# Windowed attention and maxout FFN on one core: the loads of chunk 1 and the transposes of chunk 3

## The chip, the cores and the metric

The kernel runs on one core of one Trainium2 chip. The metric is device time in microseconds (us) of one execution; lower is better. Four runs of the kernel before took 179.96, 181.50, 181.77 and 181.35 us, median 181.43.

## The reference

Four batches, eight heads, 768 tokens, head size 64; each token attends to the first four tokens ("sinks") and to a window of the last 128. The result goes through a feed-forward block whose hidden layer is the maximum of three products.

```python
def _attn_ref(q, k, v, n_sink, window):          # 4, 8, 768, 64; n_sink 4, window 128
    scores = scale * np.matmul(q, k.transpose(0, 1, 3, 2))
    is_sink = pos[None, :] < int(n_sink)
    rel = pos[:, None] - pos[None, :]
    in_window = (rel >= 0) & (rel < int(window))
    scores = np.where(is_sink | in_window, scores, -1000000000.0)
    a = np.exp(scores - np.max(scores, axis=-1, keepdims=True))
    a = a / (np.sum(a, axis=-1, keepdims=True) + 1e-09)
    return np.matmul(a, v)

def _moe_ref(x, w1, w2, w3, w_out):              # x: 3072 x 512; w1..w3: 512 x 768
    h = np.maximum(np.maximum(x @ w1, x @ w2), x @ w3)
    return h @ w_out                             # w_out: 768 x 512
```

## The kernel before

The 3072 tokens are cut into twelve chunks of 256 (three to a batch; chunks 0, 3, 6 and 9 begin one, and `CPB` is 3). For each chunk the kernel loads K, Q and V for all heads, casts them to bfloat16, turns K and Q so that the head dimension lies on partitions (`kk`, `qT`), makes scores in PSUM, exponentials (`e_sb`), a mask, products with V (`o_ps`), the normalized x (`x_sb`), its transpose (`xT`), nine FFN groups (`h_ps`, with the maximum taken by DVE) and the output product (`y_ps`).

Every engine works through its own instructions in order. That order is written out by hand: `run("Ka0 Sa01 ...", a=0)` makes the steps in the order of the words, a letter for the step, then the chunk, then an argument. K and Q turn keys and queries (on TensorE), D turns both by the DMA crossbar from SyncE's queue (`turn`), E copies the crossbar's K into its place (`place_k`), B opens score banks with the mask's terms, S makes scores and exponentials, M masks, Z and V are the sink's scores and products, A the products with V, T the transpose of x (`xpose`), F an FFN group, Y and W the output product, L a load, O a store.

There are three ways in which K and Q of a chunk get turned:

- `load` (L64 to L97) brings K and Q in four transfers of 256 KB in float32 and V in one of 512 KB, all issued on SyncE's queue (SP). `cast_qk` (L195) casts each quarter; `prep` (L225) then turns a quarter by four TensorE transposes and copies it from PSUM. The kernel before does this for chunk 0 and chunk 3.
- `load_runs` (L76) lets GpSimd's queue cast to bfloat16 in the transfer; `prep_runs` (L239) turns K or Q by 32 matmuls of 64 columns. The kernel before does this for chunks 1 and 2, with V on GpSimd's queue too.
- `turn` (L262) uses two crossbar transposes on SP, after the casts. The kernel before does this from chunk 4 on.

`xpose` (L372) uses TensorE for x of chunks 0 to 2, and the crossbar from chunk 3 on. A transfer's issue on an engine's queue waits in that queue for what it needs: a crossbar transpose on SP holds back all loads written after it until GpSimd's casts are done.

The weights (`load_w`, `load_wo`) and the loads of chunks 1 and 2 go out on GpSimd's queue, between GpSimd's own casts. The load of chunk 3 has a gate: GpSimd writes one element of its tile after the first half of the cast of V of chunk 2, so SP cannot issue it before. [...] The sink rows of V (`vs_raw`) come in four small transfers on SP, are copied by GpSimd (`v_sink`), spread by TensorE (`sink_v`) and copied from PSUM by DVE (`vs`).

Of the kernel before, what the change touches and what calls it, by code (L numbers as in the profile page):

```python
# [16 lines left out]
def kernel(  # L17
# [13 lines left out]
    nc = tc.nc  # L31
# [4 lines left out]
    d_ff = moe_w1.shape[1]  # L36
# [5 lines left out]
    CPB = S // 256  # L42
# [8 lines left out]
    with tc.manual_schedule():  # L51
# [26 lines left out]
        def load_runs(ci):  # L78

            b, c = divmod(ci, CPB)  # L80
            t0 = c * 256
            runs[ci] = raw.tile([128, 2, 16 * D], BF16, tag="runs", bufs=2, name="runs")
            for j, src in ((0, k), (1, q)):
                nc.gpsimd.dma_start(
                    out=runs[ci][:, j],
                    in_=src[b, :, t0:t0 + 256].rearrange("h (r x) d -> h r (x d)", x=16))
            raws[ci] = [None]

        def load_v(ci, eng=nc.sync):
            b, c = divmod(ci, CPB)  # L90
            t0 = c * 256
            vr = raw.tile([128, 2, H, D], F32, tag="v_raw", name="v_raw")
            eng.dma_start(
                out=vr.rearrange("p n h d -> p (n h d)").rearrange("p (h x) -> p h x", h=H),
                in_=v[b, :, t0:t0 + 256].rearrange("h (p i) d -> p h (i d)", i=2))
            raws[ci].append(vr)

        def load(ci, gate=None):
            load_qk(ci, gate)
            load_v(ci)  # L100
# [5 lines left out]
        R = H * n_sink  # L106
        vs_raw = const.tile([R, B, D], F32, name="vs_raw")
        load(0)
        for x in range(n_sink):
            nc.sync.dma_start(out=vs_raw[x * H:(x + 1) * H],  # L110
                              in_=v[:, :, x].rearrange("b h d -> h b d"))
# [12 lines left out]
        def warm(n):  # L124

            wp = psum.tile([128, 128], F32, tag="f", name="warm")
            for _ in range(n):
                nc.tensor.matmul(wp, lhsT=ident, rhs=ident, start=True, stop=True)  # L128
# [23 lines left out]
        def mask_terms(m, mb):  # L152
            nc.vector.tensor_scalar(out=mb, in0=m, scalar1=30000.0, scalar2=-30000.0,
                                    op0=ALU.mult, op1=ALU.add)
# [3 lines left out]
        def load_w(wi, lo=0, hi=d_ff):  # L158

            w = (moe_w1, moe_w2, moe_w3)[wi]  # L160
            wt = const.tile([128, DS, hi - lo], BF16, name=f"w{wi}_{lo}")
            nc.gpsimd.dma_start(out=wt, in_=w[:, lo:hi].rearrange("(a p) f -> p a f", p=128))
            for fb in range(lo // 128, hi // 128):
                w_sb[wi, fb] = wt[:, :, fb * 128 - lo:fb * 128 - lo + 128]
# [3 lines left out]
        def load_wo():  # L168
            for a in range(2):
                nc.gpsimd.dma_start(  # L170
                    out=wo[:, 3 * a:3 * a + 3],
                    in_=moe_w_out[384 * a:384 * a + 384].rearrange("(a p) f -> p a f", p=128))
# [5 lines left out]
        def sink_v_init():  # L178
            nc.gpsimd.memset(sel, 0.0)
            nc.gpsimd.memset(v_sink[:, :, D:D + 1], 1.0)  # L180
            idv = ident[0:R, 0:R].rearrange("r (s p h) -> r p s h", p=NP, h=2)
            for h in range(2):
                nc.gpsimd.tensor_copy(sel[:, h, :, 0:2 * n_sink].rearrange(
                    "r p (s h) -> r p s h", h=2)[:, :, :, h], idv[:, :, :, h])
# [10 lines left out]
        def cast_qk(ci, j, g, eng):  # L195
            if ci not in bfs:
                bfs[ci] = raw.tile([128, 2, 2, 2, 256], BF16, tag="qk_bf", name="qk_bf")
            src = raws[ci][0][:, j, g].rearrange("p (h i d) -> p h i d", h=4, d=D)
            if ci <= CPB:
                dst = bfs[ci][:, j, g]  # L200
            else:
                dst = bfs[ci][:, j].rearrange("p i a x -> p i (a x)")[:, :, 256 * g:256 * g + 256]
            (eng.tensor_copy if eng else nc.scalar.copy)(  # L203
                dst.rearrange("p i (h d) -> p h i d", d=D), src)

        def cast_v(ci, n, eng, places=(0, 1)):
            b, c = divmod(ci, CPB)
            dst = ve[b % 2][:, 2 * c + n, :, 0:D]
            vr = raws[ci][1]
            src = vr.rearrange("p n h d -> p (n h d)").rearrange("p (h i d) -> p h i d", h=H, i=2)  # L210
            for i in places:
                (eng.tensor_copy if eng else nc.scalar.copy)(  # L212
                    dst[64 * i:64 * i + 64], src[64 * n:64 * n + 64, :, i])

        def cast(ci):
            for j, g in ((0, 0), (1, 0), (0, 1), (1, 1)):
                cast_qk(ci, j, g, nc.gpsimd)
            for n in range(2):
                cast_v(ci, n, nc.gpsimd)
# [50 lines left out]
        def sink_k(b, copy=nc.scalar.copy):  # L270
            kv = ks[b % 2][:, :, 0:2 * n_sink]
            for h in range(2):
                hp = slice(64 * h, 64 * h + 64)
                for i in range(2):
                    copy(
                        kv[hp].rearrange("p a (t i h) -> p i a t h", i=2, h=2)[:, i, :, :, h],
                        kk[b * CPB % (2 * CPB)][hp, :, 64 * i:64 * i + n_sink // 2])
# [94 lines left out]
        def xpose(ci, t):  # L372
            if t == 0:
                xTs[ci] = work.tile([128, 2, DS, 128], BF16, tag="xT", bufs=3, name="xT")
            if ci >= CPB:
                nc.sync.dma_start_transpose(
                    out=xTs[ci][:, t], in_=xs[ci][:, t].rearrange("p h d -> p (h d)"))
                return
            pt = psum.tile([128, DS, 128], BF16, tag="f", name="xt_ps")
            x = xs[ci][:, t].rearrange("p h d -> p (h d)")  # L380
            for ds in range(DS):
                nc.tensor.transpose(pt[:, ds], x[:, ds * 128:(ds + 1) * 128], ident)  # L382
            copy = nc.vector.tensor_copy if ci == 0 else nc.scalar.copy
            copy(xTs[ci][:, t], pt)  # L384
# [110 lines left out]
        def run(text, **at):  # L495
            for tok in text.split():
                step(f"{tok[0]}{at[tok[1]]:02d}{tok[2:]}" if tok[1] in at else tok)

        load_runs(1)
        load_v(1, nc.gpsimd)
        load_w(0, 0, 256)
        load_w(0, 256, d_ff)
        sink_v_init()
        warm(36)
        cast_qk(0, 0, 0, nc.vector)
        cast_qk(0, 1, 0, nc.vector)
        run("Ka0", a=0)
        mask_terms(msk0, msb0)  # L510
        warm(4)
        run("Qa0 Ba01", a=0)
        cast_qk(0, 0, 1, nc.vector)
        cast_qk(0, 1, 1, nc.vector)
        mask_terms(msk, msb)
        run("Ka1 Sa01 Qa1 Ba23", a=0)
        run("Sa23", a=0)
        cast_v(0, 0, nc.vector)
        cast_v(0, 1, nc.gpsimd)
        sink_k(0, nc.gpsimd.tensor_copy)  # L520
        load_w(1, 0, 256)
        load_w(1, 256, 512)
        nc.gpsimd.tensor_copy(v_sink[:, :, 0:D], vs_raw)
        cast_v(1, 0, nc.gpsimd)
        cast_v(1, 1, nc.gpsimd)
        load_w(1, 512, d_ff)
        load_w(2)
        load_runs(2)
        load_v(2, nc.gpsimd)
        load_wo()  # L530
        warm(6)
        run("Kb0 Aa0 Aa1 Qb0 Aa2 Aa3", a=0, b=1)
        run("Sb01 Zb", b=1)
        sink_v()
        run("Ta0 Ta1 Mb01 Bb23 Sb23 Fa0 Vb Ab0 Ab1 Fa3 Ab2 Ab3 Fa6 Fa1 Fa4 Tb0 Tb1 Fa7", a=0, b=1)
        cast_v(2, 0, nc.gpsimd)
        load(3, nc.gpsimd)
        cast_v(2, 1, nc.gpsimd)
# [1 line left out]
            a=0, b=1, c=2)  # L540
        nc.gpsimd.memset(ks[1], 0.0)
        nc.gpsimd.memset(ve[1][:, :, :, D:D + 1], 1.0)
        cast(3)
        load(4)
        run("Fb5 Sc23 Mc23 Fb8 Vc Ac0 Ac1 Ya0 Ya1", a=0, b=1, c=2)
        cast(4)
        run("Ac2 Ac3 Yb0 Tc0 Tc1 Kd0 Qd0 Kd1 Qd1 Yb1", b=1, c=2, d=3)
        run("Zd Sd0123 Md0123 De Lf", d=3, e=4, f=5)


# [7 lines left out]
        for i in range(2, NCH):  # L558
            if i + 3 < NCH:
                cast(i + 3)  # L560
            if i == 2:
                text = ("Fa0 Fa1 Fa2 Vb Ab0 Fa3 Ab1 Xb Fa4 Ab2 Fa5 Ab3 Tb0 Tb1 Fa6 Dd Le Fa7 Fa8 "
                        "Ya0 Ec Ya1 Zc Sc0123 Mc0123")
            else:
                stores = " ".join(f"O{ci:02d}" for ci in outs.get(i, ()))
                text = ("Fa0 Fa1 Ec Fa2 Vb Ab0 Fa3 Xb Ab1 Fa4 Ab2 Fa5 Ab3 Tb0 Tb1 Fa6 Dd Le "
                        f"{stores} Fa7 Fa8 Zc Sc0123 Mc0123 Wa0")
            run(text, a=i, b=i + 1, c=i + 2, d=i + 3, e=i + 4)
# [38 lines left out]
```

## Time and profile before

| | |
|---|---|
| median of 4 runs | 181.43 us |
| the profiled execution | 181.42 us |
| its span, first to last instruction | 179.7 us |
| granted TensorE clock | 0.999 |
| HBM read, written | 25.20 MB, 6.29 MB |
| SP's queue (q1): packets, share of 16 DMA engines | 61696, 64.7% |
| GpSimd's queue (q0): packets, share | 5392, 17.1% |

The page gives the busy time of each engine; the span in 40 slices of 4.5 us, a digit for the busy tenths; and the chain of waits, followed back from the last instruction. PE is TensorE's matmuls, PEld its weight loads, DVE VectorE, ACT ScalarE, POOL GpSimd, SPq the queue of SyncE. A line of the timeline reads: start in us, length in us, engine, line, operation, output and inputs with shapes, count, and in brackets the idle time of that engine just before, with what ended it. With such a bracket that names a DMA, the start of the instruction is also the landing of that transfer.

### The profile page before, as it was taken

How to read it: one execution, taken by the hardware profiler on the slowest of the kernel's cores; microseconds unless marked ns; L12 is line 12 of the kernel's file. 1: busy time of each engine (PE TensorE's matmuls, PEld its weight loads, DVE VectorE, ACT ScalarE, POOL GpSimd, SP SyncE). 2: the span in 40 equal slices, each digit the busy share in tenths (PEclk: the TensorE clock that was granted, in tenths of full speed). 3: DMA queues.
4: the chain of work that ended last, by engine and by line, in shares of the span. 5: the costliest groups of instructions: out<-in, count | busy, mean ns of one | idle time of the engine just before them, and what ended most of it. 6: DMA issues, size and time to landing. Idle time of an engine off the chain costs nothing.

```text
span 179.7 us, 4863 instructions
## 1 busy us (share of the span) xinstructions
PE 169.2 (94%) x1968; PEld 130.5 (73%) x1968; DVE 117.5 (65%) x245; ACT 88.5 (49%) x187; POOL 69.5 (39%) x124
## 2 busy tenths in 40 slices
PE   6759999999999999999999999999999999999990
PEld 6526788775697688588597687686796795896880
DVE  1449762788299289767676785786686776772551
ACT  2446833373981671931934914915636627523120
POOL 7979901644925525315425335246147000000000
PEclk9999999999999999999999999999999999999999
DMA  4999999999399996598696795798997975805804
GB/s 145 236 228 204 191 206 243 224 270 253 87 149 288 129 224 172 114 230 213 116 255 160 153 274 120 157 292 211 209 293 181 205 229 107 271 35 119 287 8 117
DMA packets 67350, 34.16 MB, mean 190 GB/s; under 512 B 28832, under 2 KB 63648, under 8 KB 67328
## 3 DMA queue, kind: packets, MB, share of 16 engines
q1 hardware_dynamic: 61696, 28.22, 64.7%
q0 software_dynamic: 5392, 5.38, 17.1%
q10 hardware_dynamic: 240, 0.26, 0.6%
q8 instruction: 15, 0.25, 0.5%
q14 instruction: 7, 0.06, 0.1%
HBM read 25.20 MB, written 6.29 MB: 175 GB/s over the span
## 4 chain that ended last, share of the span: by engine, by line
PE 86%; DMA 5%; ACT 3%; POOL 2%; DVE 1%; issue 1%; POOLq 0%
PE h_ps L397 53%; PE y_ps L418 16%; PE o_ps L359 6%; DMA runs<-in_k_dram 5%; PE st L307 4%; PE y_ps L435 2%; PE pt L251 1%; ACT e_sb L313 1%; DVE h_sb L403 1%; PE o_ps L346 1%; PE sk L326 1%; PE xt_ps L382 1%; POOL msk L139 1%; ACT xT L384 1%; ACT qT L256 1%
## 5 line engine op out<-in xcount | busy, mean ns | idle before, releaser
L397 PE MATMUL h_ps<-xT,w 128*128 128x256 bf16 x864 | 103.5, 273 | 0.2
L397 PEld LDWEIGHTS <-w 128*128 128x128 bf16 x864 | 81.2, 98 | 12.0 <-issue 1.4
L403 DVE TENSOR_TENSOR h_sb<-h_sb,h_ps 128x512 bf16<-128x512 bf16 x72 | 49.1, 684 | 27.3 <-PE h_ps L397 22.0
L313 ACT ACTIVATE e_sb<-st 128x512 bf16<-128x512 f32 (+1 forms) x96 | 45.2, 589 | 7.6 <-PE st L307 7.6
L401 ACT CAST h_sb<-h_ps 128x512 bf16<-128x512 f32 x36 | 21.9, 610 | 46.3 <-PE h_ps L397 46.3
L320 DVE TENSOR_TENSOR e_sb<-e_sb,msk 128x1024 bf16<-128x1024 bf16 (+1 forms) x42 | 30.9, 750 | 16.5 <-ACT e_sb L313 16.0
L203 POOL CAST qk_bf<-qk_raw 128x512 bf16<-128x512 f32 x36 | 21.9, 611 | 46.8 <-DMA qk_raw<-in_k_dram 26.3
L212 POOL CAST ve<-v_raw 64x512 bf16<-64x512 f32 x46 | 30.6, 666 | 22.1 <-DMA v_raw<-in_v_dram 20.3
L418 PE MATMUL y_ps<-wo,h_sb 128*128 128x512 bf16 x132 | 30.6, 380 | 0.2
L418 PEld LDWEIGHTS <-h_sb 128*128 128x128 bf16 x132 | 12.4, 97 | 14.2 <-issue 1.1
L367 DVE TENSOR_TENSOR x_sb<-o_ps,rc 128x256 bf16<-128x256 f32 x48 | 20.4, 425 | 1.6
L359 PE MATMUL o_ps<-ve,e_sb 128*128 128x65 bf16 x352 | 17.7, 194 | 0.0
L424 ACT COPY y_sb<-y_ps 128x512 f32<-128x512 f32 x22 | 12.5, 632 | 9.8 <-PE y_ps L418 9.7
L359 PEld LDWEIGHTS <-e_sb 128*128 128x128 bf16 x352 | 15.5, 98 | 1.9
L408 POOL DMA_DIRECT2D out_dram<-y_sb x1 | 0.6, 571 | 35.9 <-ACT y_sb L446 35.9
L307 PE MATMUL st<-qT,kk 64*128 64x128 bf16 (+1 forms) x256 | 13.4, 238 | 0.8 <-ACT qT L256 0.4
L307 PEld LDWEIGHTS <-kk 64*128 64x128 bf16 x256 | 8.9, 94 | 5.0 <-issue 3.2
L364 DVE RECIPROCAL rc<-o_ps 128x4 f32<-128x4 f32 x48 | 8.4, 176 | 2.1 <-PE o_ps L359 2.0
L331 ACT ACTIVATE e_sink<-sk 128x256 bf16<-128x256 f32 x8 | 3.1, 393 | 7.0 <-PE sk L326 7.0
L128 PE MATMUL warm<-ident 128*128 128x128 bf16 x46 | 4.9, 293 | 1.4 <-POOL ident masks.py:199 1.4
L128 PEld LDWEIGHTS <-ident 128*128 128x128 bf16 x46 | 4.4, 138 | 1.6 <-POOL ident masks.py:199 1.4
L256 ACT CAST qT<-pt 128x512 bf16<-128x512 f32 x4 | 2.1, 588 | 6.6 <-PE pt L251 6.6
(58 smaller groups left out, 69.5 us busy)
## 6 DMA issues: line engine op xcount, KB each, us to landing
out_dram<-y_sb SPq DMA_DIRECT2D x22, 256.0 KB, 4.7
qk_raw<-in_k_dram SPq DMA_DIRECT2D x20, 256.0 KB, 4.1
qk_raw<-in_q_dram SPq DMA_DIRECT2D x20, 256.0 KB, 4.5
v_raw<-in_v_dram SPq DMA_DIRECT2D x10, 512.0 KB, 5.8
v_raw<-in_v_dram POOLq DMA_DIRECT2D x2, 512.0 KB, 9.7
w<-in_moe_w_dram POOLq DMA_DIRECT2D x4, 256.0 KB, 7.3
w<-in_moe_w_dram POOLq DMA_DIRECT2D x1, 768.0 KB, 8.5
wo<-in_moe_w_out_dram POOLq DMA_DIRECT2D x2, 384.0 KB, 12.2
```

The costliest lines, as they stand in the source:

```text
L203: (eng.tensor_copy if eng else nc.scalar.copy)(dst.rearrange("p i (h d) -> p h i d", d=D), src)
L212: (eng.tensor_copy if eng else nc.scalar.copy)(dst[64 * i:64 * i + 64], src[64 * n:64 * n + 64, :, i])
L307: nc.tensor.matmul(st[h][:, sl], lhsT=kx[r, p, k0:k0 + 128], rhs=qx[r], start=not opened, stop=True, skip_group_check=opened)
L313: nc.scalar.activation(e[:, h, lo:], st[:, lo:], AF.Exp, scale=scale)
L320: nc.vector.tensor_tensor(out=e, in0=e, in1=m, op=ALU.mult)
L359: nc.tensor.matmul(o[:, t, h], lhsT=es[ci, p][:, h, sl], rhs=ve[b % 2][:, n, 2 * p + h], start=(c == 0 and x == 0), stop=(x == len(blocks) ...
L367: nc.vector.tensor_mul(xs[ci][:, :, 2 * p:2 * p + 2], o[:, :, :, 0:D], rc.unsqueeze(3).to_broadcast([128, 2, 2, D]))
L397: nc.tensor.matmul(hp[:, f], lhsT=w_sb[wi, 2 * fp + f][:, ds], rhs=xTs[ci][:, :, ds], start=(ds == 0), stop=(ds == DS - 1))
L401: nc.scalar.copy(dst, hp)
L403: nc.vector.tensor_max(dst, dst, hp)
L418: nc.tensor.matmul(yps[ci, t], lhsT=hs[ci][:, fb, t * 128:(t + 1) * 128], rhs=wo[:, fb], start=(fb == 0), stop=(fb == FB - 1))
L424: nc.scalar.copy(y[:, t], yps.pop((ci, t)))
```

## The change

K, Q and V of chunk 1 come through `load` on SP, right behind chunk 0 and ahead of the sink rows; `load_runs(1)` and `load_v(1)` on GpSimd are gone. Chunk 1 is cast by DVE, GpSimd and ScalarE, and turned by `prep`, which also did chunk 0. In `cast_qk`, chunk 3 takes the crossbar's layout; its K and Q are turned by `D03` (SP) ahead of `load(4)`, and `Ed` replaces `Kd0 Qd0 Kd1 Qd1`. `xpose` uses TensorE for chunk 3 too. The first weights' loads move behind casts of chunk 0 on GpSimd, some casts change engines, a filler of six matmuls (`warm(6)`) goes, and the order of the words around chunks 0 and 1 and of chunk 2's round changes.

```diff
         load(0)
+        load(1)
         for x in range(n_sink):
             nc.sync.dma_start(out=vs_raw[x * H:(x + 1) * H],
...
-            if ci <= CPB:
+            if ci < CPB:
                 dst = bfs[ci][:, j, g]
...
-            if ci >= CPB:
+            if ci > CPB:
                 nc.sync.dma_start_transpose(
...
-        load_runs(1)
-        load_v(1, nc.gpsimd)
-        load_w(0, 0, 256)
-        load_w(0, 256, d_ff)
-        sink_v_init()
         warm(36)
         cast_qk(0, 0, 0, nc.vector)
-        cast_qk(0, 1, 0, nc.vector)
+        cast_qk(0, 1, 0, None)
...
         cast_qk(0, 0, 1, nc.vector)
-        cast_qk(0, 1, 1, nc.vector)
+        sink_v_init()
+        cast_qk(0, 1, 1, nc.gpsimd)
+        load_w(0, 0, 256)
         mask_terms(msk, msb)
         run("Ka1 Sa01 Qa1 Ba23", a=0)
         run("Sa23", a=0)
         cast_v(0, 0, nc.vector)
         cast_v(0, 1, nc.gpsimd)
+        load_w(0, 256, d_ff)
+        cast_qk(1, 0, 0, nc.vector)
+        cast_qk(1, 1, 0, nc.gpsimd)
         sink_k(0, nc.gpsimd.tensor_copy)
         load_w(1, 0, 256)
         load_w(1, 256, 512)
+        run("Aa0 Aa1 Kb0 Aa2 Aa3 Qb0", a=0, b=1)
+        cast_qk(1, 0, 1, nc.vector)
+        cast_qk(1, 1, 1, None)
         nc.gpsimd.tensor_copy(v_sink[:, :, 0:D], vs_raw)
-        cast_v(1, 0, nc.gpsimd)
         cast_v(1, 1, nc.gpsimd)
         load_w(1, 512, d_ff)
         load_w(2)
         load_runs(2)
         load_v(2, nc.gpsimd)
         load_wo()
-        warm(6)
-        run("Kb0 Aa0 Aa1 Qb0 Aa2 Aa3", a=0, b=1)
-        run("Sb01 Zb", b=1)
+        run("Sb01 Kb1 Qb1 Ta0 Ta1 Zb Bb23 Sb23", a=0, b=1)
+        cast_v(1, 0, nc.vector)
         sink_v()
-        run("Ta0 Ta1 Mb01 Bb23 Sb23 Fa0 Vb Ab0 Ab1 Fa3 Ab2 Ab3 Fa6 Fa1 Fa4 Tb0 Tb1 Fa7", a=0, b=1)
+        run("Mb01 Fa0 Vb Ab0 Ab1 Fa3 Ab2 Ab3 Fa6 Fa1 Fa4 Tb0 Tb1 Fa7", a=0, b=1)
...
         cast(3)
+        run("D03")
         load(4)
         run("Fb5 Sc23 Mc23 Fb8 Vc Ac0 Ac1 Ya0 Ya1", a=0, b=1, c=2)
         cast(4)
-        run("Ac2 Ac3 Yb0 Tc0 Tc1 Kd0 Qd0 Kd1 Qd1 Yb1", b=1, c=2, d=3)
+        run("Ac2 Ac3 Yb0 Tc0 Tc1 Ed Yb1", b=1, c=2, d=3)
...
             if i == 2:
-                text = ("Fa0 Fa1 Fa2 Vb Ab0 Fa3 Ab1 Xb Fa4 Ab2 Fa5 Ab3 Tb0 Tb1 Fa6 Dd Le Fa7 Fa8 "
+                text = ("Fa0 Fa1 Fa2 Vb Ab0 Fa3 Ab1 Xb Fa4 Ab2 Fa5 Ab3 Fa6 Dd Le Fa7 Tb0 Tb1 Fa8 "
                         "Ya0 Ec Ya1 Zc Sc0123 Mc0123")
```

In the words above, a to f stand for the chunks that the call names (a=0, b=1, c=2, d=3 and so on; in chunk 2's round a=2).

## The prediction

> **What bounds the kernel now.** I read the page first: busy time by engine, the slices, the chain of waits. TensorE is busy 94% and from the fifth slice on shows nines only; the chain that ended last is 86% PE. So time can be lost or won in two ways: TensorE work, or a wait of TensorE. The 5% of DMA in the chain is one wait, for K of chunk 1.
>
> ```profile
> PE 169.2 (94%) x1968; PEld 130.5 (73%) x1968; DVE 117.5 (65%) x245; ACT 88.5 (49%) x187; POOL 69.5 (39%) x124
> ...
> PE   6759999999999999999999999999999999999990
> ...
> DMA  4999999999399996598696795798997975805804
> GB/s 145 236 228 204 191 206 243 224 270 253 87 149 288 129 224 172 114 230 213 116 255 160 153 274 120 157 292 211 209 293 181 205 229 107 271 35 119 287 8 117
> ...
> PE 86%; DMA 5%; ACT 3%; POOL 2%; DVE 1%; issue 1%; POOLq 0%
> ```
>
> The DMA row matters as much: the engines are full from 4.5 us until 45 us (slices 2 to 10). Whatever the change moves in that stretch pushes something else.
>
> Then the timeline of the front (start, length, engine, line, what, and in brackets the idle time before it and who ended it):
>
> ```profile
> 8.23 0.61 DVE L203 CAST qk_bf<-qk_raw 128x512 bf16<-128x512 f32 x1 [1.62 <-DMA qk_raw<-in_q_dram]
> 10.65 1.18 DVE L212 CAST ve<-v_raw 64x512 bf16<-64x512 f32 x2 [0.76 <-DMA v_raw<-in_v_dram]
> 13.20 0.70 PE L251 MATMUL pt<-ident,runs 128*64 128x64 bf16 x32 [2.06 <-DMA runs<-in_k_dram]
> 18.47 0.62 PE L307 MATMUL st<-qT,kk 64*128 64x128 bf16 x12
> 20.22 0.66 PE L359 MATMUL o_ps<-ve,e_sb 128*128 128x65 bf16 x16
> 30.97 1.26 POOL L212 CAST ve<-v_raw 64x512 bf16<-64x512 f32 x2 [8.48 <-DMA v_raw<-in_v_dram]
> 38.71 0.61 POOL L203 CAST qk_bf<-qk_raw 128x512 bf16<-128x512 f32 x1 [1.80 <-DMA qk_raw<-in_k_dram]
> 42.78 2.61 POOL L212 CAST ve<-v_raw 64x512 bf16<-64x512 f32 x4 [2.58 <-DMA v_raw<-in_v_dram]
> 45.46 2.28 POOL L203 CAST qk_bf<-qk_raw 128x512 bf16<-128x512 f32 x4
> 47.69 1.28 POOL L212 CAST ve<-v_raw 64x512 bf16<-64x512 f32 x2
> 47.74 1.06 PE L307 MATMUL st<-qT,kk 64*128 64x256 bf16 x16
> 47.20 1.32 SPq L266 DMA_TRANSPOSE kT<-qk_bf  x1
> 58.27 0.42 DVE L223 COPY kk<-kT 128x1024 bf16<-128x1024 bf16 x1
> ```
>
> To be seen: TensorE's one long wait (2.06 us) ends at 13.20 with K of chunk 1. The next marks are the first value products of chunk 1 (Ab0) at 20.22 and the scores of chunk 3 (Sd) at 47.74. V of chunk 2 lands at 30.97; on it hangs the load of chunk 3, because its gate stands behind that cast on GpSimd. K and Q of chunk 3 are cast by 40.2 us, so in the kernel before they lie idle for 5 us until TensorE turns them (1.06 us for 16 transposes at 45.45).
>
> **The change, part by part.** The profiled execution took 181.42 us with a span of 179.7; the median of the runs is 181.43, so sums made on the profile hold for the median.
>
> *Chunk 1 on SyncE's queue.* Removed: 64 matmuls of 64 columns (2 x 0.70 us); added: 16 transposes (1.06), so 0.3 us less TensorE work. The filler of six matmuls (0.51) goes too, in a wait anyway. The wait of 2.06 us at 13.20 is what the change can win. TensorE would start earlier on chunk 0's value products, bound by V of chunk 0 at about 10.6 and its casts. But in the changed order Ab0 waits for V of chunk 1, tenth on SP's queue. When does that land? The nearest row is the train of chunks 3 and 4, the same ten transfers: first issue 32.40, last V ready at 47.69, so 15.3 us; from SP's first issue at 0.81 this gives 16.1 us, the lower bound, with no other queue in between. The first layer's weights (0.79 MB in two transfers on GpSimd's queue) now come beside it: all of them ahead of V add 0.79 MB / 229 GB/s (the rate from 9.0 to 13.5 us) = 3.4, so 19.5 is the upper bound. I take the small weight transfer whole and half of the large one (0.52 MB, 2.3 us), since GpSimd issues the second only after chunk 0's V is cast: 18.4 us. V landed at 14.7 before (8.6 us after its issue at 6.04).
>
> Behind V the changed DVE order is: two casts of V (1.18), sink values from PSUM (0.75 for two), a mask (0.64): Ab0 at 18.4 + 2.6 = 21.0, against 20.22: 0.8 late. GpSimd's side (sink V copy 0.39, two casts 1.62) ends earlier, at 20.4. The small sink-V transfers now lie behind chunk 1 on SP too, and GpSimd, then TensorE, wait for them; I add nothing, since they are 32 KB. A second chain gives a floor. ScalarE now has the cast of chunk 1's last Q ahead of the first exponentials, and stands until it has landed. In the train of chunks 3 and 4 that Q landed 6.6 after its issue at 39.50, so 13.7 after the first, here 14.5. Then 0.6 cast, 2.06 exponentials, and after them TensorE's scores (0.62), sink values (0.39), first FFN group (1.05) and sink products (0.29) in front of Ab0, with 0.1 between: 19.6, or 0.6 early. So of the 2 us wait, at best 0.6 is left at Ab0; bounds -0.6 and +1.9 (V at 19.5).
>
> [...]
>
> *GpSimd's later loads.* GpSimd does 1.3 us less casting of V but two casts of K/Q (1.2) more, and stands for V of chunk 1 before it issues the last third of w1, w2, chunk 2, and w_out. That was at 17.37; now 18.4 + 0.4 + 1.6 = 20.4, 3 us later. The cost at V of chunk 2 (30.97) lies between nothing (the queue still has bytes to move) and the 3 us. Bytes until then: 3.15 MB of chunks 0 and 1, 0.79 of w0 and 0.52 of w1, 4.46 MB; at 215 GB/s (between the slices' 236 and 191) from 2.0 on these end at 22.7, while the first new packets need some 2 us from issue (4.70 to about 7 before), so 22.4: the queue runs nearly dry but not for 3 us. The float32 of K and Q writes 0.5 MB more than the casting transfer (2.3 us if written bytes count, nothing if read bytes do). I take half, 1.5 us: V of chunk 2 at 32.5, chunk 3's V at 44.3, its third cast done at 40.8.
>
> *Chunk 3 by the crossbar.* Removed 16 transposes and their PSUM copies: 0.9 of TensorE. Added: two crossbar transposes on SP, ahead of chunk 4's five loads, which wait behind them for GpSimd's casts. The scores Sd then wait for kT, a copy of 0.42 on DVE, and qT. Lower bound: issued at 40.8 with the rows of chunk 4's pair, 5.5 and (1.4 later) 5.0 us to landing: 47.2. TensorE itself arrives at 47.74 + 0.8 - 0.9 = 47.6, so no stall. Upper bound: these transposes stand behind chunk 3's V in the same rings. Chunk 4's pair stood right behind chunk 4's V (47.69) and landed at 52.7 and 53.6, 5.9 after it: 44.3 + 5.9 = 50.2. That is the only row with a V ahead, so I take two thirds of the way, 49.2: Sd 1.5 late. [...]
>
> *What follows on SP.* Chunk 4's transposes waited in the kernel before until 47.20; from there to chunk 5's last cast (57.8) were 10.6 us, one period of transposes, load, casts. From 40.8 this gives 51.4 for chunk 4, landed by 57.8 (needed at 58.27 + 1.5), and 62.0 for chunk 5, kT at 66.9 with the row's 4.8 (needed at 66.37 + 1.5). Covered, with 1 us to spare; a further 2 us late cost about that.
>
> *x of chunk 3 by TensorE.* Eight transposes, 0.61 from the row at 45.01, pipelined some 0.5: on the path, since TensorE is full there. The two PSUM copies lie behind w_out's matmuls. The casts moved from DVE to ScalarE and GpSimd for chunk 0 cost nothing: ScalarE sat idle 4.0 us there.
>
> Sum: Sd +1.5, x +0.5, so +2.0: 181.42 + 2.0 = 183.4 us.
>
> **The rivals.** (a) *Not slower:* the front's win survives. V of chunk 1 lands by 17.0 or earlier, Ab0 is 0.6 early, GpSimd's queue does not run dry, and the crossbar does not wait for V. Sd is then TensorE's own: 47.74 - 0.6 - 0.9 = 46.2 (kT and qT at 45.7), -1.5, with x +0.5: 180.4. It decides from V at 17.0 on (17.0 + 2.6 = the floor). For: chunk 0's V landed 9.8 us after SP's first issue although GpSimd's loads had started. Against: DMA at nine tenths throughout. (b) *Nothing to measure:* the front is as I say, but the transposes pass V: TensorE's own arrival, 47.6, plus x 0.5: 181.8. This is also the case that the crossbar brings nothing as 16 transposes were hidden or not. (c) *The queue runs dry:* all 3 us reach chunk 2 and 3, V of chunk 3 at 45.8, qT at 51.7, Sd +4.0, x +0.5: 185.9, and the next transposes no longer have spare.
>
> **How the numbers follow.** Forecast (182.2 to 184.8) 0.42; (a) 0.15; (b) 0.20; (c) 0.23. Below 1% (1.8 us, about what a measurement tells from no change) cannot be told. Faster, under 179.6: the lower half of (a), 0.08. Within, to 183.2: the rest of (a), (b), and a quarter of the forecast, 0.38. Slower: the rest, 0.54. The range leaves out half of (a) and the upper part of (c): 180.4 to 186.3.
>
> **What would show it.** In the changed profile: the cast of V of chunk 1 on DVE waits for DMA until about 18.4; Ab0 near 21; V of chunk 2 on GpSimd near 32.5; the first transposes of K issued near 40.8, landing 8 us later; PE idle of 1 to 2 us before Sd, at the copy of kk or at qT. I am wrong if V of chunk 1 is there by 17, or if Sd starts without a wait.

## The result: no change that can be measured, and the profile after

The changed kernel took 181.07 us in the median of 36 runs, the kernel before 181.34 in 55; the ratio is 1.0013, 95% interval 0.9994 to 1.0033. The ratio leaves out the runs of each kernel that took over 1.5% more than its fastest, so it is not the quotient of the two medians. The forecast of 183.4 us was wrong. The profiled execution took 180.18 us with a span of 178.5 (before: 181.42 and 179.7).

From the page after: busy time, TensorE's slices, DMA's slices, the chain.

```profile
PE 169.4 (95%) x1906; PEld 130.2 (73%) x1906; DVE 118.5 (66%) x247; ACT 89.0 (50%) x188; POOL 70.8 (40%) x121
...
PE   6959999999999999999999999999999999999991
...
DMA  4999999989998991796996997898998986815804
...
PE 81%; DVE 8%; DMA 3%; ACT 2%; issue 1%; SPq 1%; POOL 1%; DVEq 0%; POOLq 0%
```

TensorE's second slice (4.5 to 9.0 us) goes from 7 to 9. The third, in which TensorE waited for K of chunk 1 before, stays at 5: that one wait is gone, but TensorE is hardly busier there. Its busy time over the run is the same too (169.4 against 169.2), and in the chain DVE's share has gone from 1% to 8%. That is the first hint of what took the wait's place.

Three more marks of the kernel before, the first scores of chunk 1, the FFN group Fa3 and the scores of chunk 4:

```profile
15.90 0.62 PE L307 MATMUL st<-qT,kk 64*128 64x128 bf16 x12 [0.44 <-ACT qT L256]
20.72 1.04 PE L397 MATMUL h_ps<-xT,w 128*128 128x256 bf16 x8
60.46 0.78 PE L307 MATMUL st<-qT,kk 64*128 64x128 bf16 x16
```

The same marks from the timeline of the changed kernel (the line numbers are one higher in the lines shown):

```profile
13.11 0.62 PE L308 MATMUL st<-qT,kk 64*128 64x128 bf16 x12 [0.67 <-ACT qT L237]
13.98 0.62 PE L234 MATMUL pt<-ident,qk_bf 128*128 128x128 bf16 x8 [0.25 <-DVE qk_bf L204]
15.74 0.86 DVE L213 CAST ve<-v_raw 64x512 bf16<-64x512 f32 x2
17.27 0.77 DVE L192 CAST vs<-vs_ps 128x260 bf16<-128x260 f32 x2 [0.66 <-PE vs_ps L190]
18.79 0.42 PE L360 MATMUL o_ps<-ve,e_sb 128*128 128x65 bf16 x8 [0.23 <-DVE e_sb L321]
19.39 0.41 PE L360 MATMUL o_ps<-ve,e_sb 128*128 128x65 bf16 x8 [0.19 <-DVE e_sb L321]
19.64 1.04 PE L398 MATMUL h_ps<-xT,w 128*128 128x256 bf16 x8
31.46 1.26 POOL L213 CAST ve<-v_raw 64x512 bf16<-64x512 f32 x2 [8.19 <-DMA v_raw<-in_v_dram]
43.70 0.48 DVE L224 COPY kk<-kT 128x1024 bf16<-128x1024 bf16 x1
45.77 1.06 PE L308 MATMUL st<-qT,kk 64*128 64x256 bf16 x16
59.24 0.89 PE L308 MATMUL st<-qT,kk 64*128 64x128 bf16 x19
```

Chunk 1's first scores start at 13.11 (15.90 before), its first value products, Ab0, at 18.79 (20.22), the next FFN group, Fa3, at 19.64 (20.72), chunk 3's scores, Sd, at 45.77 (47.74), chunk 4's at 59.24 (60.46). V of chunk 1 landed 7.4 us after its issue at 7.88, at 15.3; DVE's cast of it waits for nothing. The copy of kT at 43.70 does not wait either. Read as a pair, the two profiles say 1.2 us faster; the times of many runs say nothing changed. Both have to be explained.

### The profile page after: what moved, and what is told of

Same layout as the page of the kernel before. It is cut to its first block, busy times and chain, and to the rows that moved or that the text cites. A ratio compares the mean times of both kernels' runs of the same rounds, so it can differ in the third digit from the quotient of the medians.

```text
span 178.5 us, 4750 instructions
## 1 busy us (share of the span) xinstructions
PE 169.4 (95%) x1906; PEld 130.2 (73%) x1906; DVE 118.5 (66%) x247; ACT 89.0 (50%) x188; POOL 70.8 (40%) x121
## 4 chain that ended last, share of the span: by engine, by line
PE 81%; DVE 8%; DMA 3%; ACT 2%; issue 1%; SPq 1%; POOL 1%; DVEq 0%; POOLq 0%
PE h_ps L398 49%; PE y_ps L419 17%; PE o_ps L360 6%; PE st L308 4%; DVE h_sb L404 3%; DMA v_raw<-in_v_dram 3%; DVE x_sb L368 2%; PE y_ps L436 2%; ACT e_sb L314 1%; SPq L70 1%; PE sk L327 1%; PE o_ps L347 1%; PE xt_ps L383 1%; POOL ve L213 1%; DVE e_sb L321 1%
## 5 line engine op out<-in xcount | busy, mean ns | idle before, releaser
L321 DVE TENSOR_TENSOR e_sb<-e_sb,msk 128x1024 bf16<-128x1024 bf16 (+1 forms) x42 | 31.7, 767 | 17.4 <-ACT e_sb L314 16.7
L204 POOL CAST qk_bf<-qk_raw 128x512 bf16<-128x512 f32 x38 | 24.7, 653 | 40.9 <-DMA qk_raw<-in_k_dram 30.7
L213 POOL CAST ve<-v_raw 64x512 bf16<-64x512 f32 x44 | 31.1, 707 | 24.5 <-DMA v_raw<-in_v_dram 15.9
L425 ACT COPY y_sb<-y_ps 128x512 f32<-128x512 f32 x22 | 12.6, 632 | 8.7 <-PE y_ps L419 8.7
L163 POOL DMA_DIRECT2D w<-in_moe_w_dram x6 | 4.8, 810 | 0.0
```

Source lines behind the costliest of these rows:

```text
L204: (eng.tensor_copy if eng else nc.scalar.copy)(dst.rearrange("p i (h d) -> p h i d", d=D), src)
L213: (eng.tensor_copy if eng else nc.scalar.copy)(dst[64 * i:64 * i + 64], src[64 * n:64 * n + 64, :, i])
L321: nc.vector.tensor_tensor(out=e, in0=e, in1=m, op=ALU.mult)
L425: nc.scalar.copy(y[:, t], yps.pop((ci, t)))
```

## The experiments

All ratios are against runs of the kernel before on the same chip. The table gives the marks, in us, of one profiled execution of each kernel. "Half clock" is the stretch in which TensorE's granted clock was 0.5 in the front (the end of the run aside).

| kernel | scores of 1 | Ab0 | Fa3 | Sd | scores of 4 | half clock | ratio (interval) |
|---|---|---|---|---|---|---|---|
| before | 15.90 | 20.22 | 20.72 | 47.74 | 60.46 | none | 1 |
| before again | 15.53 | 22.29 | 22.79 | 49.81 | 62.54 | 6.8 us | |
| chunk 3 part alone | 14.85 | 19.17 | 19.66 | 45.79 | 59.16 | none | 0.9983 (0.9942 to 1.0024) |
| crossbar for K, Q alone | 15.09 | 20.10 | 20.60 | 46.72 | 59.78 | 3.4 us | 1.0012 (0.9970 to 1.0054) |
| changed | 13.11 | 18.79 | 19.64 | 45.77 | 59.24 | none | 1.0013 (0.9994 to 1.0033) |
| changed again | 13.21 | 19.48 | 20.34 | 46.46 | 59.83 | 3.4 us | 0.9983 (0.9947 to 1.0020) |
| front part alone | 13.25 | 19.57 | 20.43 | 47.45 | 60.17 | none | 1.0006 (0.9977 to 1.0035) |

**The changed kernel and the kernel before once more**, both unchanged.

> The changed kernel, unchanged, for a second profile and more times beside the same runs of the kernel before. Theory 1 (the first profile, 178.5 us of span with Ab0 at 18.8 and the scores of chunk 3 at 45.8, is typical; the win is real but given back later): again Ab0 near 18.8 and Sd near 45.8, V of chunk 1 at about 15.3, ratio to before 0.993 to 1.003. Theory 2 (the first profile was a lucky execution, V of chunk 1 lands at different times from one execution to the next): V of chunk 1 0.7 us or more later, Ab0 at 19.5 or later, span 179.2 or more.

> The kernel before once more, for a third look at its front (Ab0 at 20.22 and 19.17 in two executions of the same front). If its first profile was a late execution: Ab0 at 19.2 to 19.7, K of chunk 1 at 12.1 to 12.7, span 178.8 to 179.3. If it was typical: Ab0 at 20 or later, span 179.5 or more.

The second execution of the changed kernel had V of chunk 1 at 15.4 again, but Ab0 at 19.48 and a span of 178.9; its granted clock was 0.5 from 12.6 to 16.0 us, where TensorE was busy for 2.79 of 3.40 us; that this makes most of the 0.7 us is my estimate. The second execution of the kernel before had 6.8 us of half clock, and TensorE works through its front in 2 us more; it says nothing about the undisturbed front. Neither theory of these two runs holds as stated: V lands at the same time, and the front still moves by 0.7 to 2 us between executions. One profile of each kernel cannot tell 1 us here. These lines are the second execution of the kernel before by stages (length; busy time and count of PE, PEld, DVE, ACT, POOL; granted clock; DMA share; GB/s):

```profile
11.00:14.40 3.40, 1.58 (x74) 1.49 (x76) 1.09 (x2) 0.18 (x1) 2.49 (x8) 1.00 1.17 251
14.40:21.20 6.80, 6.74 (x70) 3.81 (x65) 5.05 (x15) 3.93 (x9) 5.90 (x9) 0.50 1.33 190
```

**The two parts, each alone.** The front alone is the changed kernel without these:

```diff
-            if ci < CPB:
+            if ci <= CPB:
...
-            if ci > CPB:
+            if ci >= CPB:
...
-        run("D03")
...
-        run("Ac2 Ac3 Yb0 Tc0 Tc1 Ed Yb1", b=1, c=2, d=3)
+        run("Ac2 Ac3 Yb0 Tc0 Tc1 Kd0 Qd0 Kd1 Qd1 Yb1", b=1, c=2, d=3)
```

(with the words of chunk 2's round as before too); the chunk 3 part is the kernel before with just those edits the other way round.

> The front of the change alone: chunk 1 on SyncE's queue, chunk 3 as in the kernel before (K and Q turned by TensorE, x by the crossbar). Theory 1 (the front wins 1.4 us at Ab0 and keeps it): Ab0 near 18.8, Sd near 46.7 (47.7 less 1.4, plus what DMA is late), ratio 0.992 to 0.995. Rival (the front's win is lost again where chunk 2 or chunk 3 waits for DMA): Ab0 near 18.8 but PE idle of 1 us or more before Kc0, Kd0 or the scores of chunk 4, ratio 0.998 to 1.003.

> The other part alone: chunk 1 as in the kernel before, K and Q of chunk 3 by the crossbar, x of chunk 3 by TensorE. Theory 1 (the 16 transposes saved are 0.9 us of TensorE, the eight added cost 0.5 to 0.9, so this part is worth nothing): Sd near 46.8 without a wait, the first scores of chunk 4 within 0.4 us of 60.5, ratio 0.998 to 1.002. Rival (the crossbar is late, or the later loads of chunks 4 and 5 stall DVE at kk): Sd at 47.7 or later or an idle DVE before kk, ratio 1.003 to 1.01.

Both are level with the kernel before. The chunk 3 part has the front of the kernel before, and in an execution without half clock:

```profile
12.15 0.70 PE L251 MATMUL pt<-ident,runs 128*64 128x64 bf16 x32 [2.03 <-DMA runs<-in_k_dram]
14.85 0.62 PE L307 MATMUL st<-qT,kk 64*128 64x128 bf16 x12 [0.44 <-ACT qT L256]
19.17 0.66 PE L359 MATMUL o_ps<-ve,e_sb 128*128 128x65 bf16 x16
19.66 0.60 PE L397 MATMUL h_ps<-xT,w 128*128 128x256 bf16 x4
45.79 1.06 PE L307 MATMUL st<-qT,kk 64*128 64x256 bf16 x16
59.16 1.18 PE L307 MATMUL st<-qT,kk 64*128 64x128 bf16 x24
```

This shows where the pair of profiles misled. The old front, wait of 2.03 us included, reaches Fa3 at 19.66 here; the changed front got there at 19.64, and at 20.43 in the front part alone. In the first execution of the kernel before, the last quarter of chunk 0's Q was cast at 8.23, while the three other executions of that front had it at 7.3 to 7.4; that execution was about 1 us late from the start.

The two stages behind Fa3 hardly depend on what the front did. Fa3 to Sd takes 27.02 where TensorE turns K and Q of chunk 3 (before, before again, front alone), 26.12 to 26.13 where the crossbar does: 0.9 us won, as priced. Sd to the scores of chunk 4 takes 12.72 in the first three and 13.37 to 13.47 where x goes through TensorE: 0.65 to 0.75 lost. (In two of the runs below this stretch was 0.1 to 0.2 us longer, 12.95 and 13.59.) Further back the executions differ again. The front part alone stood once more behind the last mark of the table, at x of a later chunk, whose transposes go through the crossbar in every kernel here; its time of 182.55 us holds this wait, which no other execution of the table has there:

```profile
128.33 2.78 PE L398 MATMUL h_ps<-xT,w 128*128 128x256 bf16 x24 [1.27 <-DMA xT<-x_sb]
```

Where does the front's win go? The scores of chunk 1 start 1.7 us earlier than in the chunk 3 part, and at Fa3 nothing is left. Busy times by engine from 9.0 to 19.6 us, the changed kernel first, the chunk 3 part (old front) second; columns as above:

```profile
9.00:19.60 10.60, 8.11 (x122) 5.29 (x122) 9.14 (x25) 8.20 (x18) 8.22 (x16) 1.00 1.29 237
```

```profile
9.00:19.60 10.60, 8.13 (x176) 5.69 (x175) 6.69 (x18) 7.35 (x17) 9.61 (x20) 1.00 1.25 213
```

TensorE does the same work in the same time: 8.11 and 8.13 us. DVE, third, goes from 6.69 to 9.14 of 10.60 us: it now casts K and V of chunk 1 and copies its q. The wait of 2 us is cut into waits for other engines (0.63 and 0.20 for the casts of V, 0.30, 0.67 and 0.25 for casts and copies of K and Q, 0.23 and 0.19 for masks in the first profile), and half of chunk 1's transposes now stand behind its first scores.

**Crossbar for K and Q of chunk 3 alone**: the chunk 3 part with x left on the crossbar, chunk 1 on GpSimd's queue; and **the changed kernel with x of chunk 3 back on the crossbar**. Both come from this edit, on the chunk 3 part alone and on the changed kernel, with the words of chunk 2's round as before too:

```diff
-            if ci > CPB:
+            if ci >= CPB:
                 nc.sync.dma_start_transpose(
```

> The kernel before with K and Q of chunk 3 turned by the crossbar ahead of chunk 4's load and nothing else (x of chunk 3 stays on the crossbar, chunk 1 on GpSimd's queue). Theory (it saves 16 transposes, 0.9 us, and nothing waits): from Ab0 to Sd 26.6 us as in the run of the chunk 3 part, from there to the scores of chunk 4 12.7, ratio 0.993 to 0.997. Rival (SyncE's queue, with two transposes more ahead of chunk 4, brings x of chunk 3 or kk of chunk 5 late): a wait of 0.7 us or more between 60 and 80 us, ratio 0.998 to 1.004.

> The changed kernel with x of chunk 3 turned by the crossbar as in the kernel before (and the words of chunk 2's round as before). Theory (the eight transposes are the 0.65 to 0.75 us that all kernels with x by TensorE take longer from the scores of chunk 3 to those of chunk 4, 13.4 against 12.7): 12.7 us again, ratio 0.994 to 0.998. Rival (the transposes of x now wait on SyncE's queue behind a late load, and chunk 3's FFN or chunk 5's kk waits for them): the time from Sd to the first scores of chunk 4 stays at 12.7 but PE or DVE idles 0.7 us or more between 60 and 75 us, ratio 0.998 to 1.005.

The 0.9 us were there again (26.12 from Fa3 to Sd), but the first gained nothing, and the second was slower: 1.0115 (1.0057 to 1.0173). The stretch from Sd to the scores of chunk 4 did not go back to 12.7 but to 13.07, and behind it, in the second kernel, stands a wait that the kernel before does not have:

```profile
62.16 2.02 PE L398 MATMUL h_ps<-xT,w 128*128 128x256 bf16 x17 [1.49 <-DMA xT<-x_sb]
```

Chunk 3's first FFN group waits for the transposes of x, issued at 56.05 right behind the load of chunk 5, which the crossbar transposes of chunk 3 have made late (its V is issued at 55.43; before, at 53.01). So the two halves of the chunk 3 part belong together: x goes to TensorE to keep off SyncE's queue. In the first kernel TensorE stood 0.72 us at 75.33, put down to ScalarE; whether that was the transposes of x too is open.

**When does kT of chunk 3 land?** Its copy moved ahead of chunk 2's value products:

```diff
-        run("Fb5 Sc23 Mc23 Fb8 Vc Ac0 Ac1 Ya0 Ya1", a=0, b=1, c=2)
+        run("Fb5 Sc23 Mc23 Fb8 Ed Vc Ac0 Ac1 Ya0 Ya1", a=0, b=1, c=2, d=3)
-        run("Ac2 Ac3 Yb0 Tc0 Tc1 Ed Yb1", b=1, c=2, d=3)
+        run("Ac2 Ac3 Yb0 Tc0 Tc1 Yb1", b=1, c=2, d=3)
```

> The changed kernel with the copy of the turned K of chunk 3 (Ed) put ahead of chunk 2's value products, so that DVE must wait for the crossbar and shows when kT of chunk 3 lands. The forecast's reading (transposes held behind V of chunk 3): DVE waits until 5 us after that V, 47.5 or later. Rival (they pass it, or go between its packets): the copy starts 3 to 5.5 us after the issue of kT, at 42 to 45, with V of chunk 3 landing at about the same time. The run is slower by what DVE stands; no time is read from it.

From the timeline of that kernel, SyncE's issue, GpSimd's cast of V of chunk 3, DVE's copy of kT:

```profile
38.89 1.32 SPq L267 DMA_TRANSPOSE kT<-qk_bf  x1
```

```profile
42.19 2.69 POOL L213 CAST ve<-v_raw 64x512 bf16<-64x512 f32 x4 [2.20 <-DMA v_raw<-in_v_dram]
```

```profile
43.20 0.55 DVE L224 COPY kk<-kT 128x1024 bf16<-128x1024 bf16 x1 [2.08 <-DMA kT<-qk_bf]
```

kT lands 4.3 us after its issue and 1.0 after V, not 5. The rival holds.

**Are the two queues' transfers shared out?** Both loads of the first layer's weights ahead of everything, as in the kernel before:

```diff
+        load_w(0, 0, 256)
+        load_w(0, 256, d_ff)
         warm(36)
...
-        load_w(0, 0, 256)
...
-        load_w(0, 256, d_ff)
```

> The changed kernel with both loads of the first layer's weights issued on GpSimd's queue before anything else of the front, as in the kernel before, so that 0.79 MB goes beside chunks 0 and 1 from about 6.5 us on. If the two queues share the DMA engines evenly (the forecast's reading): V of chunk 0 lands some 1.5 us later than 8.98, V of chunk 1 3.4 us later, at 17.5 to 19, Ab0 at 20 to 21.5, ratio 1.004 to 1.012 against before. Rival (SyncE's queue goes first in fact, GpSimd's transfers only fill what is left): V of chunk 1 within 0.7 us of 15.3, Ab0 near 18.8, ratio as the changed kernel's.

V of chunk 1 landed 11.3 us after its issue at 7.8, at 19.1, 3.8 us later than in the changed kernel, and the second quarter of chunk 1 before it:

```profile
14.93 0.61 PE L234 MATMUL pt<-ident,qk_bf 128*128 128x128 bf16 x4 [3.25 <-POOL qk_bf L204]
```

The ratio is 1.027 (1.022 to 1.032); 10.2 us of half clock add to what this profile shows (Ab0 24.84), so its time is not all the weights'. The half clock alone did not make V late in the changed kernel's second execution (from 12.6 to 16.0 us, V at 15.4 against 15.3); here the two queues moved data side by side: by the packets in the trace, from 8.0 to 14.0 us GpSimd's queue moved 0.77 MB and SyncE's 0.62. The 3.8 us is more than my price: 3.4 us was meant for all of the weights against none, and in the changed kernel 0.46 MB of them had already gone before V landed. V of chunk 0 was not late, as I had expected (its cast on GpSimd starts at 9.03): the weights are issued at 4.70, but their first packet starts at 7.9.

**The sink rows**, in two other places: ahead of V of chunk 1 on SyncE's queue, and on ScalarE's queue at the start, the latter with the whole change and with the front part alone.

```diff
-        load(1)
+        load_qk(1)
         for x in range(n_sink):
             nc.sync.dma_start(out=vs_raw[x * H:(x + 1) * H],
...
+        load_v(1)
```

```diff
-            nc.sync.dma_start(out=vs_raw[x * H:(x + 1) * H],
+            nc.scalar.dma_start(out=vs_raw[x * H:(x + 1) * H],
```

> The changed kernel with one edit: the four small transfers of the sink rows go out on SyncE's queue ahead of V of chunk 1 instead of behind it (K and Q of chunk 1 still first). In three executions of the changed front DVE stood 0.66, 0.75 and 1.25 us in front of the copy of the sink values, whose matmul waits for GpSimd's copy of those rows. Theory (the sink rows, which the forecast priced at nothing, set Ab0 in the changed front): the copy of sink values starts before V's cast is done, DVE does not stand there, Ab0 at 18.2 to 18.8 (0.7 us or more less than the mean of 19.3), ratio to before 0.993 to 0.998. Rival (V of chunk 1, now later on the queue, or GpSimd's cast of it takes the place of the rows): Ab0 at 19.0 or later, ratio 0.997 to 1.003.

> The changed kernel with the four transfers of the sink rows issued by ScalarE at the very start instead of by SyncE behind chunk 1; nothing else on SyncE's queue moves. Theory (in the changed front the sink rows arrive last, DVE's copy of the sink values and with it the masks and Ab0, Ab1 wait for them): no wait of DVE before the copy of the sink values, V of chunk 1 still at 15.3 to 15.8, Ab0 near 18.2 and the second FFN group (Fa3) at 18.9 to 19.4 instead of 19.6 to 20.4, ratio to before 0.994 to 0.999. Rival (the masks wait for V's cast on DVE and GpSimd's cast anyway): Fa3 at 19.6 or later, ratio 0.998 to 1.003.

> The front part alone (chunk 3 as in the kernel before) with the sink rows issued by ScalarE at the start. Theory: against the front part alone (Fa3 at 20.4, time 181.6) Fa3 at 19.4 or earlier, ratio to before 0.996 to 1.000. Rival: as the front part alone, 1.000 to 1.004.

Ahead of V they are worse, 1.0050 (1.0017 to 1.0082): V lands at 17.24, and DVE waits 1.23 us for it.

```profile
17.27 1.18 DVE L214 CAST ve<-v_raw 64x512 bf16<-64x512 f32 x2 [1.23 <-DMA v_raw<-in_v_dram]
```

On ScalarE's queue DVE's wait before the copy of the sink values shrank from 0.66 to 0.36 us (now TensorE's own order), V was there at 15.2, and Fa3 still came at 19.64; ratio 0.9977 (0.9933 to 1.0020), and with the front part alone 0.9995 (0.9956 to 1.0034; its profiled execution had 6.8 us of half clock, so its Fa3, at 21.59, tells nothing). So the sink rows are not what holds the front; the rival holds.

**TensorE's wait before the scores of chunk 1, filled** with the second half of K (and the sink rows on ScalarE's queue):

```diff
-        run("Aa0 Aa1 Kb0 Aa2 Aa3 Qb0", a=0, b=1)
+        run("Aa0 Aa1 Kb0 Aa2", a=0, b=1)
         cast_qk(1, 0, 1, nc.vector)
+        run("Aa3 Qb0 Kb1", a=0, b=1)
...
-        run("Sb01 Kb1 Qb1 Ta0 Ta1 Zb Bb23 Sb23", a=0, b=1)
+        run("Sb01 Qb1 Ta0 Ta1 Zb Bb23 Sb23", a=0, b=1)
```

> The changed kernel with the sink rows issued by ScalarE and the second half of K of chunk 1 cast and turned before the first scores of chunk 1, in TensorE's wait for ScalarE's copy of qT (0.67 us in every execution of this front). Theory (the front's win of some 1.6 us at the first scores of chunk 1 is eaten by small waits for casts and PSUM copies and by chunk 1's second half, which now follows the scores): the wait before the scores gets shorter by the four transposes (0.2), the wait behind them (0.25 to 0.57) goes, Fa3 at 19.0 to 19.3 instead of 19.6, ratio to before 0.992 to 0.998. Rival (what bounds Ab0 is DVE's row of copies and masks, whatever TensorE does): Fa3 at 19.5 or later, DVE without a wait over 0.2 us from 13 to 18.5 us, ratio 0.996 to 1.002.

Fa3 at 19.91, ratio 0.9983 (0.9937 to 1.0029). The wait has only moved to the transposes:

```profile
13.79 0.40 PE L234 MATMUL pt<-ident,qk_bf 128*128 128x128 bf16 x4 [1.13 <-DVE qk_bf L204]
```

From 9.0 to 19.9 us DVE was busy for 9.58 of 10.90. It stood twice, 0.45 and 0.36 us, more than the rival allowed, but what TensorE waits for is DVE's cast.

## Why the prediction was wrong

The step that failed is the wait at Sd: crossbar transposes held up behind V of chunk 3, 1.6 us beyond TensorE's own arrival. That wait did not exist. Both signs that the prediction had named for being wrong came: V of chunk 1 was there by 17 (at 15.3), and Sd started without a wait. Point by point:

- **V of chunk 1 at 18.4.** Wrong: 15.2 to 15.8 in the executions with that order on the queues, below even the lower bound of 16.1. The bound was made on the train of chunks 3 and 4, which started while w_out's transfer was still on the way (landed at 34.6, two microseconds after the train's first issue). Whether that alone made the train slow was not tested. I also took 0.52 MB of the weights as moving ahead of V; the run with the weights early shows the two queues sharing where both have transfers waiting (0.77 and 0.62 MB from 8.0 to 14.0 us). In the changed order GpSimd issues them at 7.73 and 10.57, but their first packet starts at 10.4, when 2.4 of the 3.2 MB on SyncE's queue had moved. By V's landing 0.46 MB of weights had gone, near the 0.52 that I had taken. So it is the bound of 16.1, not the share of the weights, that was too late.
- **Ab0 at 21.0, 0.8 late.** It came at 18.7 to 19.6 in the executions of the changed front without half clock. At the next FFN group, Fa3, these stand at 19.55 to 20.43 against 19.66 of the old front: 0.1 early to 0.8 late. The mechanism I named, DVE's row of V cast, sink values and masks, is the one that the runs show, but as the tax on a win, not as a wait for V: DVE is nearly full there (9.14 of 10.60 us).
- **V of chunk 2 at 32.5.** At the upper end of what came, 30.9 to 32.5 in the executions with the changed front (34.7 with the weights early), against 30.5 to 30.9 in those of the old without half clock. It has room, as the trace of before showed: landed by 30.97, first used by value products at 40.14.
- **Sd 1.5 late, held by transposes behind V.** This is the step that failed, and the largest term: 0.8 for the front, less 0.9 for the transposes saved, plus 1.6 of waiting. I took two thirds of the way to "5.9 after V", from the one row in which transposes followed a V. That row's 5.0 and 5.9 us were counted from V by chance of the moment: there the transposes were issued 0.5 us before V's cast began, so their own 5.5 us told the same story. With the changed front kT was issued 1.5 to 3.8 us ahead of V's landing, and it landed 4.2 to 5.5 us after its issue in the executions that show it. In the run with the early copy it was there at 43.2, and in the changed kernel Sd started at 45.77 without a wait for it or for qT, where I had 49.2. TensorE waited for nothing, and the 0.9 us of the 16 transposes came in full.
- **x by TensorE, 0.5.** Right in kind, 0.65 to 0.75 in size. I had not seen why it was needed: without it chunk 3 waits 1.5 us for the crossbar.
- **Chunks 4 and 5 covered on SyncE's queue.** TensorE did not wait for kT or qT of either in the changed kernel: their scores start at 59.24 and 70.25 with no idle time before them.

Added up on executions without half clock: front -0.1 to +0.8, K and Q -0.9, x +0.7, so -0.3 to +0.6 us: no change that can be told, as the 36 runs say. The last section shows that the runs at full clock lie in this range, at +0.3 to +0.5. Of the rivals, (b) came nearest in what it says: V does not hold the transposes, and its sum of 181.8 is the forecast without the wait. Its front was 0.8 late, as mine; the runs have -0.1 to 0.8. Rival (a), the front's win surviving, did not come true. Not shown is that DVE alone is the limit: no run took work from DVE in the front without moving it to another engine on the same path. The change that would tell, chunk 1's casts on an engine with room, was not tried; ScalarE (8.20 of 10.60) and GpSimd (8.22) have little.

## What to carry to other kernels

Here the removal of a wait of 2 us brought nothing that could be measured, with DVE, next in line, busy for 9.14 of 10.60 us: before pricing such a wait, add up the busy time of every engine in the stretch up to the next mark, with the moved work in it. Where transfers move, count a landing from its own issue and from rows in which the queue is as full as it will be; an interval to whatever else landed nearby is no price (kT came 4.3 us after its issue and 1.0 after V, where the interval said 5). And with executions that differ by 1 us, a second profile of each kernel is worth more than a closer look at the first. The granted clock of every timed run belongs beside its time.

## What the runs showed that was not expected

The granted TensorE clock is cut to 0.5 in some executions, with the same program: in 5 of the 14 profiled executions, for 3.4, 6.8 or 10.2 us, starting between 10.9 and 14.4 us. With 3.4 us of it the changed kernel had Ab0 0.7 us later (19.48 against 18.79), with 6.8 us the kernel before 2.1 later (22.29 against 20.22), and no row of a profile without it shows that it can happen. In the 3.4 us ahead of each such stretch (the length of the shortest) TensorE was busy for 1.08 to 1.97 us, 32 to 58%. But the first profile of the kernel before had 1.34 busy of the 3.4 us up to 13.5, and no cut. What sets it off is not shown.

The timed runs tell how often each front is cut. In the profiled executions the mean granted clock was 0.995 to 1.000 without such a stretch in the front and 0.972 to 0.991 with one, and no timed run of these two kernels lies between 0.991 and 0.995. By this, 59 of the 86 runs of the kernel before that stand beside the experiments had a cut, and 16 of 48 of the changed kernel; in the one round that had both, 24 of 29 and 6 of 12. All six runs with the weights early, where TensorE stood 3.25 us at a stretch, had one. So the changed front is cut less often; that its shorter waits are the reason was not tested.

Without a cut the changed kernel comes out slower: a mean of 181.02 us in 32 runs against 180.56 in 26 of the kernel before (medians 181.03 and 180.70; one run of 434.78 us left out), and 181.05 in 6 against 180.39 in 5 in the round that had both. Of the kernel before, runs with one cut took about 0.7 us more in the median. So the equal times of the result look like a small loss against fewer cuts; no run holds the clock fixed to prove it. The same runs also explain the pair of profiles: without a cut, only one run of the kernel before took longer than its first profiled execution (181.42), and 27 of the 32 of the changed kernel took longer than its own (180.18).
